# A Fourier filter feeding a soft mixture of experts: loads, stage-1 units and read-backs of the first batches placed by slot, TensorE's order written out

## The chip, the cores and the metric

The kernel runs on one core of one Trainium2 chip. The metric is the device time of one execution in microseconds (us). TensorE is called PE, VectorE DVE, ScalarE ACT, GpSimd POOL; SP is the engine that issues nearly all DMAs.

## The reference

`x` is 8 x 2496 x 256, the filter has 1249 x 256 complex values, and the experts are 8 with 4 slots each and 1024 hidden units. All is float32.

```python
X = np.fft.rfft(x, axis=1)
y = np.fft.irfft(X * (filt_r + 1j * filt_i), n=2496, axis=1)      # each batch, each of 256 columns
t = y.reshape(8 * 2496, 256)
logits = t @ phi                                                   # 19968 x 32
d = softmax of logits over the tokens;  slot_input = d.T @ t       # 32 x 256
slot_out[e] = relu(slot_input[e] @ w1[e]) @ w2[e]
c = softmax of logits over the 32 slots
out = c @ slot_out                                                 # 19968 x 256
```

## The kernel before

A length of 2496 is 39 x 64, and the transform is done in two stages. **Stage 1** works in units of two column blocks of 117 rows: 11 units for each of 8 batches (`split_x` and `s1_unit`). For batch 0 a unit is one float32 matmul of 512 columns (two passes on PE). For the others `split_x` has ACT round x to a reduced float32 (`xh`, L291) and POOL subtract the rest (`xl`, L292), and the unit is three matmuls of the reduced type (L308). The result is copied out of PSUM (`at`, L310 or L312) and written to DRAM (`a_dram`).

**Stage 2** reads `a_dram` back in another layout (`load_ash`, tile `ash`, five buffers) and works in slots: 10 for each batch, 80 in all. Slot n is one `x_unit`: eight PE instructions (L338), two multiplies by the filter on DVE (L352, L353), and an add and a subtract on DVE and POOL (L355, L356). Two slots later `t_unit` transposes the result (L364, copied by ACT at L366) and, every second time, forms logits (L375). Once a group of batches is through, a `chain` takes its logits through an inverse transform and the token softmax and sums `slot_input`; its steps are interleaved with the slots that follow. Batches 0 and 1 are the first group, so that no chain begins before slot 21. After slot 79 come the expert weights' loads, the experts and the combination, whose stores end the kernel.

x comes in chunks of four blocks (two units, 512 KB; six chunks a batch, the last with one unit), in three buffers `xt`; batch 0's x lies in a tile of its own. The filter tables `ff_t` come in ten loads of 256 KB; `sign_tables` multiplies the second half of each by a sign on DVE (L612), with signs made by 20 instructions on PE (`make_signs`, L604).

What sets the order: the program is written slot by slot, and a planner then orders each engine's instructions by a simulated timeline, as far as dependences let it. Where `behind` is called the order is that of the text: for every DMA on SP up to slot 24 (`issue`, `PIN`), and on PE for batch 0's units, the sign matmuls and the matmuls that only keep PE running (`keep_warm`: `WM` at the start, `WK` behind batch 0). ACT, DVE and POOL are ordered by the planner throughout.

The stage-1 units from unit 4 of batch 1 on (`EARLY = 4`; units 0 to 3 go before slot 0) are spread evenly: `slot_of` puts 73 units over 65 slots. `split_next(n + 1)` splits the units of the next slot, and after every second unit `next_x()` issues the next chunk. A batch's read-backs start two slots after its last stage-1 unit at the earliest.

Of the kernel before, what the change touches and what calls it, by code (L numbers as in the profile page):

```python
# [17 lines left out]
BATCH, SEQ, DIM = 8, 2496, 256  # L18
N1, N2 = 39, 64
NT = 20  # L20
NI = 22
NH = 11
# [16 lines left out]
P = 128  # L39
# [6 lines left out]
XB = 3  # L46
AB = 5
EARLY = 4
SPAN = 65
ASH = 5  # L50
LT = 2
HOPS = 2
RT = 1
PR = 2
FB = 1
WM = 1
WK = 2
PIN = 24
FIRST = (0, 2, 6, 10, 14, 18, 22)
PA = 6  # L60
YB = 34
# [4 lines left out]

def slot_of(b, u):

    k = (b - 1) * NH + u - EARLY
    return k * SPAN // ((BATCH - 1) * NH - EARLY) if k >= 0 else -1  # L70


def freq_of(t, c):
# [133 lines left out]
def fft_soft_moe(ctx, tc, x, ff, phi, w1, w2, cst, w1q, out):  # L207
# [24 lines left out]
    def C(name, lo=0, hi=None):  # L232
        o, rows, cols = OFF[name]
        hi = cols if hi is None else hi
        return cst_t[0:rows, o + lo : o + hi]
# [22 lines left out]
    def behind(kind, ins):  # L258
        if kind in queue:
            info = mybir.DependencyInfo(mybir.DependencyClass.NoSync, mybir.DependencyReason.DATA)  # L260
            tc.add_manual_dep(ins.ins, queue[kind].ins.name, info, reason="order of issue")
        queue[kind] = ins

    def issue(dst, src):
        ins = sp.dma_start(dst, src)
        if pinned[0]:
            behind("sp", ins)

    def keep_warm(n):
        for k in range(n):  # L270
            behind("pe", pe.matmul(pw, warm[:, 0:P], warm, start=True, stop=True))
# [10 lines left out]
    def split_x(b, u):  # L282

        if b < FB:
            xhl[b, u] = x0_t[0:KR, 2 * u : 2 * u + 2, :], None
            return
        c, k = divmod(2 * u, XC)
        xs = xts[b, c][0:KR, k : k + 2, :]
        xh = proda.tile([KR, 2, DIM], F32R, tag="xh", name=f"xh{b}_{u}", bufs=3)
        xl = proda.tile([KR, 2, DIM], F32R, tag="xl", name=f"xl{b}_{u}", bufs=3)  # L290
        act.copy(xh, xs)  # L291
        pool_e.tensor_tensor(out=xl, in0=xs, in1=xh.bitcast(F32), op=ALU.subtract)  # L292
        xhl[b, u] = xh, xl
# [3 lines left out]
    def s1_unit(b, u):  # L297
        if u == 0:
            a_dram[b] = scr.tile([N2, QR, DIM], F32, tag="a_dram", name=f"a_dram{b}")
        xh, xl = xhl.pop((b, u))  # L300
        ps = ps_s1.tile([QP, 2, DIM], F32, tag="s1", name=f"s1_{b}_{u}")
        if xl is None:
            at = ypool.tile([QP, 2, DIM], F32, tag="y", name=f"at{b}_{u}")
            behind("pe", pe.matmul(ps, w1q_t, xh, start=True, stop=True))  # L304
        else:
            at = proda.tile([QP, 2, DIM], F32, tag="at", name=f"at{b}_{u}", bufs=AB)
            for n, (w, xx) in enumerate(((w1h, xh), (w1l, xh), (w1h, xl))):
                pe.matmul(ps, w, xx, start=(n == 0), stop=(n == 2))  # L308
        if b == 0 and u % 2 == 1:
            dve.tensor_copy(at, ps)  # L310
        else:
            act.copy(at, ps)  # L312
        k0 = PK * 2 * u
        if u < NH - 1:
            issue(a_dram[b][k0 : k0 + 2 * PK].rearrange("(i j) q d -> (j q) i d", j=PK), at)
        else:
            issue(a_dram[b][k0 : k0 + PK].rearrange("j q d -> (j q) d"), at[:, 0, :])
            issue(a_dram[b][k0 + PK], at[0:QR, 1, :])
# [12 lines left out]
    def x_unit(b, c):  # L331

        t0 = 2 * c
        ash = ashs.pop((b, c))
        ps = ps_x.tile([P, 4, 2, 64], F32, tag="x", name=f"x_{b}_{c}")
        for k in range(2):
            for dh in range(2):
                pe.matmul(  # L338
                    ps[:, 2 * k + dh].rearrange("q r c -> q (r c)"),
                    ash[:, k, dh * P : (dh + 1) * P],  # L340
                    C("b1" if t0 + k else "b0"),
                    start=True,
                    stop=True,
                )
        frv, fiv = (
            ff_t[:, c, k].rearrange("q (p o c) -> q p o c", o=1, c=64).broadcast_to([P, 4, 2, 64]) for k in range(2)
        )
        t2 = prod.tile([P, 4, 2, 64], F32, tag="t2", name=f"t2_{b}_{c}")
        if c % 2 == 0:
            yts[b, c // 2] = prod.tile([P, 2, 4, 2, 64], F32, tag="yt", name=f"yt_{b}_{c}")  # L350
        yt = yts[b, c // 2][:, c % 2]
        dve.tensor_tensor(out=yt, in0=ps, in1=frv, op=ALU.mult)  # L352
        dve.tensor_tensor(out=t2, in0=ps[:, :, ::-1, :], in1=fiv, op=ALU.mult)  # L353
        add = pool_e if b >= PA else dve
        add.tensor_tensor(out=yt[:, :, 1, :], in0=yt[:, :, 1, :], in1=t2[:, :, 1, :], op=ALU.add)  # L355
        pool_e.tensor_tensor(out=yt[:, :, 0, :], in0=yt[:, :, 0, :], in1=t2[:, :, 0, :], op=ALU.subtract)  # L356

    def t_unit(b, c):

        yt = yts[b, c // 2]  # L360
        pt = ps_t.tile([P, 2, 2, P], F32, tag="t", name=f"t_{b}_{c}")
        for k in range(2):
            for dh in range(2):
                pe.transpose(pt[:, k, dh, :], yt[:, c % 2, 2 * k + dh].rearrange("q r c -> q (r c)"), ident)  # L364
        y = ypool.tile([P, 2, DIM], F32, tag="y", name=f"y_{b}_{c}")
        act.copy(y, pt.rearrange("k p h d -> k p (h d)"))  # L366
        ys[b, c] = y
        if c % 2 == 1:
            i = c // 2
            if i == 0:  # L370
                lts[b] = work.tile([P, 5, P], F32, tag="lt", name=f"lt_{b}", bufs=2)
            pl = ps_t.tile([P, P], F32, tag="t", name=f"l_{b}_{i}")
            for dh in range(2):
                for j in range(4):
                    pe.matmul(  # L375
                        pl[32 * j : 32 * j + 32, :],
                        phi_t[:, dh, :],
                        yt[:, j // 2, 2 * (j % 2) + dh].rearrange("q r c -> q (r c)"),
                        start=(dh == 0),
                        stop=(dh == 1),  # L380
                    )
            act.copy(lts[b][:, i, :], pl)

# [209 lines left out]
    def load_tables(c):  # L593
        issue(ff_t[:, c], ff[:, c])
# [25 lines left out]

    xnext = [(b, c) for b in range(1, BATCH) for c in range(6)]

    def next_x():
        if xnext:
            load_x(*xnext.pop(0))

    def split_next(n):
        for b, u in at_slot.get(n, ()):
            split_x(b, u)
            if u % 2 == 1 or u == NH - 1:  # L630
                next_x()

    x0_t = x0p.tile([P, NI, DIM], F32, name="x0_t")
    for i0, i1 in zip(FIRST, FIRST[1:]):
# [11 lines left out]
    for u in range(NH):  # L646
        if u + 1 < NH:
            split_x(0, u + 1)
        s1_unit(0, u)
        if u in (3, 7):  # L650
            next_x()
        if u == 2:
            tc.keep_in_program_order(act.dma_start(cst_t[:, 0:NEAR], cst[:, 0:NEAR]))
        if u == 4:
            tc.keep_in_program_order(act.dma_start(phi_t, phi.rearrange("(h q) e -> q h e", q=P)))
# [4 lines left out]
    def load_to(n):  # L660
        while loads:
            b, c = loads[0]
            if n < max(b * CPB + c - (3 if b < 2 else ASH), slot_of(b, NH - 1) + 2 if b else -3):
                break
            load_ash(*loads.pop(0))

    keep_warm(WK)
    next_x()
    load_tables(next(tabs_next))
    load_to(-3)  # L670
    load_tables(next(tabs_next))
    make_signs()
    for u in range(EARLY):
        split_x(1, u)
        s1_unit(1, u)
        if u % 2 == 1:
            next_x()
            load_to(-2 + u // 2)
    sign_tables(0)
    split_next(0)  # L680
    late = list(tabs_next)
# [42 lines left out]
    for n in range(NS + LT):  # L724
        if n == PIN:
            pinned[0] = False
        if n < NS:
            if late:
                load_tables(late.pop(0))
            load_to(n)  # L730
            if n == CPB + 4:
                issue(cst_t[:, NEAR:FAR], cst[:, NEAR:FAR])
            if n == NS - 2 * CPB:
                behind("sp", sp.dma_start(cst_t[:, FAR:], cst[:, FAR:]))
            if n + 1 < CPB:
                sign_tables(n + 1)
            split_next(n + 1)
            x_unit(*divmod(n, CPB))
        for b, u in at_slot.get(n, ()):
            s1_unit(b, u)  # L740
        if n == last_s1:
            proda_cm.__exit__(None, None, None)
            late_cm, lp = open_pool("late", WL, "right")
            late_pool.append(lp)
            wl = iter(range(WL))
        if n > last_s1 and next(wl, None) is not None:
            load_ws(late_pool[0], "w", 1)
        if n >= LT:
            b, c = divmod(n - LT, CPB)
            t_unit(b, c)  # L750
            if c == CPB - 1 and b in last:
                active.append((last[b], chain(last[b])))
        hop_slot(n)
# [185 lines left out]
```

## Time and profile before

| | us |
|---|---|
| median of 3 runs | 403.64 (401.32 to 404.34) |
| the profiled execution, its own time | 403.31 |
| its span | 401.5 |
| PE busy | 364.6 (91%) |
| DVE busy | 263.6 (66%) |
| ACT busy | 213.1 (53%) |
| POOL busy | 202.1 (50%) |
| granted clock of PE, mean | 0.95 |
| bytes moved by DMA | 109.09 MB, mean 272 GB/s |

The span runs from the first to the last instruction of the profile. Busy time of PE is partly modelled, since matmuls are pipelined. In the rows of single instructions the columns are start, duration, engine, line, operation, and what it writes and reads; a bracket gives the idle time ahead of it and what ended that. `x8` at a row's end means eight instructions merged. "SPq" is the issue of a DMA, not its transfer. `s` is a stage-1 result in PSUM, `x` a stage-2 one.

### The profile page before, as it was taken

What the parts mean: (1) busy time and instruction counts of PE and PEld (TensorE: products, weight loads), DVE (VectorE), ACT (ScalarE), POOL (GpSimd) and SP (SyncE); (2) the same over time, 40 slices, a digit from 0 to 9 for tenths busy, and PEclk for the clock granted to TensorE, in tenths of its full rate; (3) what the DMA queues carried; (4) which work ended last, traced back from release to release, by engine and by line L of the source; (5) the groups of instructions that cost most, each with busy time, mean ns of one, the idle gap of its engine ahead of it and who ended that gap; (6) DMA issues with size and microseconds to landing.
All of it is one profiled execution on the core that took longest, in us unless ns stands there. A gap on an engine that the chain in (4) does not pass through costs nothing.

```text
span 401.5 us, 11478 instructions
## 1 busy us (share of the span) xinstructions
PE 364.6 (91%) x4569; PEld 282.0 (70%) x4569; DVE 263.6 (66%) x460; ACT 213.1 (53%) x453; POOL 202.1 (50%) x229
## 2 busy tenths in 40 slices
PE   8977989998999999999988999999998999998960
PEld 2445767887878876877877688887675834787850
DVE  1223998778689974967899185899349432586640
ACT  2355656676576946655675734444365521475530
POOL 0266688797668674846875535565170004350000
PEclk9998999999999999999999999999999899998555
DMA  8999999899889866976898773352169999299996
GB/s 282 325 307 369 395 362 353 285 297 348 251 271 304 277 216 207 287 237 178 285 315 243 208 241 101 109 153 73 39 225 365 349 258 299 105 414 416 417 416 282
DMA packets 59691, 109.09 MB, mean 272 GB/s; under 512 B 5538, under 2 KB 34338, under 8 KB 57462
## 3 DMA queue, kind: packets, MB, share of 16 engines
q1 hardware_dynamic: 59092, 108.01, 80.0%
q8 instruction: 36, 0.59, 0.6%
q10 hardware_dynamic: 546, 0.35, 0.3%
q14 instruction: 17, 0.14, 0.1%
HBM read 65.60 MB, written 42.74 MB: 270 GB/s over the span
## 4 chain that ended last, share of the span: by engine, by line
PE 62%; DVE 14%; DMA 9%; POOL 4%; issue 4%; ACT 2%; SPq 1%; DVEq 0%; POOLq 0%; ACTq 0%
PE x L338 15%; PE s L308 9%; PE t L364 7%; PE s L558 5%; DMA out<-ob 4%; PE l L375 4%; PE out L890 3%; DMA xt<-in_x 3%; POOL xl L292 3%; PE s L304 3%; PE dd L527 2%; DVE yt L352 2%; DVE t L353 2%; PE o L857 2%; DVE yt L355 2%
## 5 line engine op out<-in xcount | busy, mean ns | idle before, releaser
L292 POOL TENSOR_TENSOR xl<-xt,xh 117x512 fp32r<-117x512 f32 x77 | 104.7, 1372 | 38.9 <-ACT xh L291 35.7
L338 PE MATMUL x<-cst_t,ash 128*128 128x128 f32 x640 | 89.6, 281 | 2.8 <-issue 2.3
L338 PEld LDWEIGHTS x<-cst_t,ash 128*128 128x128 f32 x640 | 81.0, 192 | 12.5 <-issue 7.2
L356 POOL TENSOR_TENSOR yt<-yt,t 128x256 f32<-128x256 f32 x80 | 66.0, 826 | 44.5 <-DVE t L353 35.0
L352 DVE TENSOR_TENSOR yt<-x,ff_t 128x512 f32<-128x512 f32 x80 | 54.6, 682 | 29.2 <-PE x L338 27.6
L312 ACT COPY at<-s 120x512 f32<-120x512 f32 x83 | 48.6, 587 | 27.2 <-PE s L308 16.1
L366 ACT COPY y<-t 128x512 f32<-128x512 f32 x80 | 46.1, 592 | 29.8 <-PE t L364 28.0
L291 ACT CAST xh<-xt 117x512 fp32r<-117x512 f32 x77 | 46.3, 623 | 25.3 <-PE s L308 11.0
L353 DVE TENSOR_TENSOR t<-x,ff_t 128x512 f32<-128x512 f32 x80 | 54.3, 678 | 0.0
L364 PE MATMUL t<-cst_t,yt 128*128 128x128 f32 x320 | 48.5, 276 | 3.2 <-POOL yt L356 2.6
L355 DVE TENSOR_TENSOR yt<-yt,t 128x256 f32<-128x256 f32 x60 | 46.2, 781 | 0.8
L364 PEld LDWEIGHTS t<-cst_t,yt 128*128 128x128 f32 x320 | 36.8, 141 | 10.6 <-POOL yt L356 5.0
L308 PE MATMUL s<-xh,w1h 117*120 117x512 f32 x77 | 36.1, 469 | 4.7 <-ACT xh L291 2.9
L890 PE MATMUL out<-so,st 32*128 32x256 f32 x468 | 35.3, 354 | 2.8 <-ACT ob L895 1.5
L890 PEld LDWEIGHTS out<-so,st 32*128 32x128 f32 x468 | 31.6, 234 | 6.2 <-ACT ob L895 2.6
L895 DVE COPY ob<-out 128x512 f32<-128x512 f32 (+1 forms) x40 | 25.4, 671 | 11.2 <-PE out L890 7.9
L308 PE MATMUL s<-xl,w1h 117*120 117x512 f32 x77 | 32.1, 422 | 0.6 <-POOL xl L292 0.6
L895 ACT COPY ob<-out 128x512 f32<-128x512 f32 (+1 forms) x40 | 21.7, 584 | 17.7 <-PE out L890 12.1
L308 PE MATMUL s<-xh,w1l 117*120 117x512 f32 x77 | 30.6, 398 | 0.0
L355 POOL TENSOR_TENSOR yt<-yt,t 128x256 f32<-128x256 f32 x20 | 15.6, 779 | 26.9 <-DVE t L353 19.9
L375 PE MATMUL l<-yt,phi_t 128*32 128x128 f32 x640 | 27.0, 279 | 1.0 <-issue 0.9
L796 POOL TENSOR_TENSOR c<-cl,r_all 117x352 f32<-117x352 f32 x8 | 6.2, 796 | 41.5 <-DMA cl<-c_dram 33.0
(107 smaller groups left out, 484.1 us busy)
## 6 DMA issues: line engine op xcount, KB each, us to landing
ash<-a_dram SPq DMA_DIRECT2D x80, 256.0 KB
a_dram<-at SPq DMA_DIRECT2D x80, 240.0 KB
xt<-in_x SPq DMA_DIRECT2D x35, 512.0 KB
out<-ob SPq DMA_DIRECT2D x17, 1024.0 KB
w<-in_w SPq DMA_DIRECT2D x64, 256.0 KB
x_t<-in_x SPq DMA_DIRECT2D x5, 512.0 KB
ff_t<-in_ff SPq DMA_DIRECT2D x10, 256.0 KB
out<-ob SPq DMA_DIRECT2D x5, 512.0 KB
```

The source lines that it names most:

```text
L291: act.copy(xh, xs)
L292: pool_e.tensor_tensor(out=xl, in0=xs, in1=xh.bitcast(F32), op=ALU.subtract)
L308: pe.matmul(ps, w, xx, start=(n == 0), stop=(n == 2))
L312: act.copy(at, ps)
L338: pe.matmul(ps[:, 2 * k + dh].rearrange("q r c -> q (r c)"), ash[:, k, dh * P : (dh + 1) * P], C("b1" if t0 + k else "b0"), start=True, st ...
L352: dve.tensor_tensor(out=yt, in0=ps, in1=frv, op=ALU.mult)
L353: dve.tensor_tensor(out=t2, in0=ps[:, :, ::-1, :], in1=fiv, op=ALU.mult)
L355: add.tensor_tensor(out=yt[:, :, 1, :], in0=yt[:, :, 1, :], in1=t2[:, :, 1, :], op=ALU.add)
L356: pool_e.tensor_tensor(out=yt[:, :, 0, :], in0=yt[:, :, 0, :], in1=t2[:, :, 0, :], op=ALU.subtract)
L364: pe.transpose(pt[:, k, dh, :], yt[:, c % 2, 2 * k + dh].rearrange("q r c -> q (r c)"), ident)
L890: nc.tensor.matmul(prs[k][:, mm, :], sts[n][q, hs, c0 : c0 + P], so[q, ho], start=(i == 0), stop=(i == 2))
L895: copy(ob[:, nm * k : nm * (k + 1), :], prs[k])
```

## The change

It places the early work by slot.

- `slot_of`: batch 1's remaining seven units go one to a slot into slots 0 to 6; batch 2's go into slots 8 (two of them) to 17; a later batch b starts min(b, 5) slots before slot 10(b-1) and takes one unit a slot, two in its last. Before, the units of batch 2 lay in slots 6 to 15.
- `next_x(n)`: a chunk is issued in slot n when its first unit is at most two slots away (batches 1 and 2) or four (later ones), behind that slot's table load and read-backs; before, it followed the split that frees its buffer. In the opening the first chunk of batch 1 is issued after unit 5 of batch 0 instead of unit 3, the second after batch 0's last unit instead of unit 7, the third after two table loads and two read-backs.
- The first two early units are computed around the first table and the first read-back; then come a table, a read-back, the signs, a chunk, the other two early units and the third read-back.
- The four early units use one plain float32 matmul each (two passes), without `split_x`'s cast and subtract, and their copies out alternate between ACT and DVE.
- `line`: the matmuls of stage 1, stage 2, the transposes and the logits stand on PE in the order of the text up to slot 20 (`PEPIN`). The chain's are not in that order.
- Batch 2's read-backs may start one slot after its last unit instead of two.
- One more keep-warm matmul at the start (`WM = 2`), none behind batch 0 (`WK` is gone).

```diff
-SPAN = 65
+AHEAD = 5
-WM = 1
-WK = 2
+WM = 2
 PIN = 24
+PEPIN = 20
...
 def slot_of(b, u):
-    k = (b - 1) * NH + u - EARLY
-    return k * SPAN // ((BATCH - 1) * NH - EARLY) if k >= 0 else -1
+    if b == 1:
+        return max(u - EARLY, -1)
+    if b == 2:
+        return NT // 2 - 2 + max(u - 1, 0)
+    return (b - 1) * (NT // 2) + min(u, NT // 2 - 1) - min(b, AHEAD)
...
+    in_line = [True]
+    def line(ins):
+        if in_line[0]:
+            behind("pe", ins)
...
         xs = xts[b, c][0:KR, k : k + 2, :]
+        if b == 1 and u < EARLY:
+            xhl[b, u] = xs, None
+            return
...
-        if xl is None:
+        if b == 0:
             at = ypool.tile([QP, 2, DIM], F32, tag="y", name=f"at{b}_{u}")
-            behind("pe", pe.matmul(ps, w1q_t, xh, start=True, stop=True))
         else:
             at = proda.tile([QP, 2, DIM], F32, tag="at", name=f"at{b}_{u}", bufs=AB)
+        if xl is None:
+            line(pe.matmul(ps, w1q_t, xh, start=True, stop=True))
+        else:
             for n, (w, xx) in enumerate(((w1h, xh), (w1l, xh), (w1h, xl))):
-                pe.matmul(ps, w, xx, start=(n == 0), stop=(n == 2))
-        if b == 0 and u % 2 == 1:
+                line(pe.matmul(ps, w, xx, start=(n == 0), stop=(n == 2)))
+        if xl is None and u % 2 == 1:
             dve.tensor_copy(at, ps)
...
-    def next_x():
-        if xnext:
+    def next_x(n=None):
+        while xnext:
+            b, c = xnext[0]
+            if n is not None and n < slot_of(b, 2 * c) - (2 if b < 3 else 4):
+                break
             load_x(*xnext.pop(0))
+            if n is None:
+                break
     def split_next(n):
         for b, u in at_slot.get(n, ()):
             split_x(b, u)
-            if u % 2 == 1 or u == NH - 1:
-                next_x()
...
         s1_unit(0, u)
-        if u in (3, 7):
+        if u == 5:
             next_x()
...
-            if n < max(b * CPB + c - (3 if b < 2 else ASH), slot_of(b, NH - 1) + 2 if b else -3):
+            if n < max(b * CPB + c - (3 if b < 2 else ASH), slot_of(b, NH - 1) + (1 if b == 2 else 2) if b else -3):
...
-    keep_warm(WK)
     next_x()
     load_tables(next(tabs_next))
+    for u in range(2):
+        split_x(1, u)
+    s1_unit(1, 0)
     load_to(-3)
+    s1_unit(1, 1)
     load_tables(next(tabs_next))
+    load_to(-2)
     make_signs()
-    for u in range(EARLY):
+    next_x()
+    for u in range(2, EARLY):
         split_x(1, u)
         s1_unit(1, u)
-        if u % 2 == 1:
-            next_x()
-            load_to(-2 + u // 2)
+    load_to(-1)
...
+        if n == PEPIN:
+            in_line[0] = False
         if n < NS:
             if late:
                 load_tables(late.pop(0))
             load_to(n)
+            next_x(n)
```

The matmuls of `x_unit` and `t_unit` are wrapped in `line(...)` in the same way.

More of the change, by code (lines that the diff above doesn't have):

```diff
@@ L337, in x_unit @@
             for dh in range(2):
[L338 to L343, printed above, removed]
+                line(
+                    pe.matmul(
+                        ps[:, 2 * k + dh].rearrange("q r c -> q (r c)"),
+                        ash[:, k, dh * P : (dh + 1) * P],
+                        C("b1" if t0 + k else "b0"),
+                        start=True,
+                        stop=True,
+                    )
                 )
@@ L363, in t_unit @@
             for dh in range(2):
-                pe.transpose(pt[:, k, dh, :], yt[:, c % 2, 2 * k + dh].rearrange("q r c -> q (r c)"), ident)
+                line(pe.transpose(pt[:, k, dh, :], yt[:, c % 2, 2 * k + dh].rearrange("q r c -> q (r c)"), ident))
         y = ypool.tile([P, 2, DIM], F32, tag="y", name=f"y_{b}_{c}")
@@ L374, in t_unit @@
                 for j in range(4):
[L375 to L380, printed above, removed]
+                    line(
+                        pe.matmul(
+                            pl[32 * j : 32 * j + 32, :],
+                            phi_t[:, dh, :],
+                            yt[:, j // 2, 2 * (j % 2) + dh].rearrange("q r c -> q (r c)"),
+                            start=(dh == 0),
+                            stop=(dh == 1),
+                        )
                     )
```

## The prediction, made before the change was run

> **What bounds the kernel now.** I read the page's own lines first, then the table by stretches of time, then the chain that ended last, then the order of single instructions in the opening.
>
> ```profile
> span 401.5 us, 11478 instructions
> PE   8977989998999999999988999999998999998960
> PEclk9998999999999999999999999999999899998555
> DMA  8999999899889866976898773352169999299996
> ```
>
> The reader sees TensorE (PE) at nine tenths or more in nearly every slice, and slices 3 and 4 (20 to 40 us) at seven, one of them with a lowered clock. The profiled execution took 403.31 us by its own time: 401.5 of span and 1.8 around it. The median of the three runs shown is 403.64, so the sum below, made against 403.31, stands 0.3 us under it.
>
> ```profile
> 17.20:28.20 11.00, 8.72 (x47) 6.30 (x46) 0.93 (x2) 7.25 (x14) 6.78 (x6) 1.00 0.94 309
> 28.20:39.20 11.00, 7.47 (x36) 5.28 (x35) 3.96 (x9) 5.42 (x10) 7.36 (x7) 0.84 1.02 354
> 39.20:63.80 24.60, 22.52 (x195) 17.90 (x192) 22.87 (x32) 16.12 (x32) 19.66 (x18) 1.00 1.03 379
> 63.80:90.30 26.50, 25.88 (x241) 21.60 (x241) 20.75 (x34) 17.01 (x35) 23.24 (x22) 1.00 0.91 303
> 90.30:290.00 199.70, 192.91 (x2756) 155.94 (x2755) 153.03 (x249) 116.39 (x244) 122.84 (x123) 1.00 0.70 218
> ```
>
> The columns are the length, then PE, weight loads, VectorE (DVE), ScalarE (ACT), GpSimd (POOL), the granted clock, DMA share and GB/s. The cuts are at DVE's first multiply of slots 0, 2, 10 and 20 (a slot is one `x_unit`):
>
> ```profile
> 28.26 0.69 DVE L352 TENSOR_TENSOR yt<-x,ff_t 128x512 f32<-128x512 f32 x1
> 35.05 0.69 DVE L352 TENSOR_TENSOR yt<-x,ff_t 128x512 f32<-128x512 f32 x1 [5.05 <-PE x L338]
> 39.15 0.69 DVE L352 TENSOR_TENSOR yt<-x,ff_t 128x512 f32<-128x512 f32 x1 [1.32 <-PE x L338]
> 63.84 0.68 DVE L352 TENSOR_TENSOR yt<-x,ff_t 128x512 f32<-128x512 f32 x1
> 90.27 0.69 DVE L352 TENSOR_TENSOR yt<-x,ff_t 128x512 f32<-128x512 f32 x1
> ```
>
> So there are three regimes. From 17 to 39 us DMA is full (0.94 and 1.02) and PE works 16.2 of 22 us: slots 0 and 1 take 10.9 us together. Slots 2 to 9 take 24.7 us, 3.09 each, with DVE busy 22.87 of 24.6. From slot 10 on PE is the bound: 25.88 of 26.5 us, and 192.9 of 199.7 after that, with DMA at 0.70. Whatever PE work is ready sooner there comes out sooner, and that stretch runs to the tail, so what the first 64 us give I carry to the end one for one. The ceiling is PE's idle time up to slot 20: 2.3, 3.5, 2.1 and 0.6 us in the four stretches, 8.5 in all, and whatever the lowered clock stretched.
>
> **The opening, where the change acts.**
>
> ```profile
> 15.98 6.03 DMA xt<-in_x
> 25.79 6.30 DMA xt<-in_x
> 15.98 0.91 SPq L265 DMA_DIRECT2D xt<-in_x  x1
> 16.99 3.19 SPq L265 DMA_DIRECT2D a_dram<-at  x4
> 23.97 0.33 SPq L265 DMA_DIRECT2D ash<-a_dram  x1
> 17.21 1.14 ACT L291 CAST xh<-xt 117x512 fp32r<-117x512 f32 x2 [1.35 <-DMA xt<-in_x]
> 18.26 0.58 ACT L312 COPY at<-s 120x512 f32<-120x512 f32 x1
> 27.06 1.16 PE L338 MATMUL x<-cst_t,ash 128*128 128x128 f32 x8
> 32.84 0.49 PE L308 MATMUL s<-xh,w1h 117*120 117x512 f32 x1 [1.54 <-ACT xh L291]
> 33.40 1.62 PE L338 MATMUL x<-cst_t,ash 128*128 128x128 f32 x8
> L292 POOL TENSOR_TENSOR xl<-xt,xh 117x512 fp32r<-117x512 f32 x77 | 104.7, 1372 | 38.9 <-ACT xh L291 35.7
> ```
>
> The first two are pieces of the chain. An x chunk (0.52 MB) is issued at 15.98, in front of the last four writes of batch 0, and the read-back of slot 0 is issued only at 23.97, when those writes have landed. At 25.79 another chunk is issued that lands 6.30 us later. PE waits for its cast (32.84), and slot 1's eight matmuls, which need no x, stand behind that one; they then take 1.62 us, against 1.16 for slot 0's eight at 27.06.
>
> **What the change does there, and the sum.** The second chunk goes behind batch 0's writes. At the 309 GB/s of that stretch 0.52 MB are 1.7 us, so I put the first read-back at 22.3. Casts no longer stand before the copy at 18.26 (1.14 us), because the four early units need none; that lies within the same wait and isn't added. From the issue at 23.97 to DVE's multiply at 28.26 are 4.3 us, so slot 0 starts at 26.6. In the pinned order slot 1 comes after unit (1,4), which needs the third chunk. I place its issue near 24.0, after two read-backs, two tables and two writes. Its landing has bounds from rows: 3.1 us (a read-back of half its size, issued at 23.97, was in use at 27.06) to 6.3. I take 4.0, nearer the short end, since a chunk less is ahead of it. With a cast (0.6, half of the 1.14) and a subtract (1.37) that is 30.0, slot 1 on DVE at 31.4 and slot 2 at 34.2, against 39.15: **-5.0 us**, with bounds -2.7 and -5.9.
>
> ```profile
> 43.83 0.42 DVE L355 TENSOR_TENSOR yt<-yt,t 128x256 f32<-128x256 f32 x1
> 46.35 1.44 DVE L355 TENSOR_TENSOR yt<-yt,t 128x256 f32<-128x256 f32 x1
> 47.72 0.95 DVE L612 TENSOR_TENSOR ff_t<-ff_t,sg 128x256 f32<-128x256 f32 x1
> 44.80 2.71 POOL L292 TENSOR_TENSOR xl<-xt,xh 117x512 fp32r<-117x512 f32 x2
> 47.47 0.92 POOL L356 TENSOR_TENSOR yt<-yt,t 128x256 f32<-128x256 f32 x1
> ```
>
> **Slots 2 to 9.** DVE has the same instructions per slot: two multiplies, an add, a sign table. The add takes 0.42 us alone and 1.44 under a pair of POOL's subtracts; the sign table 0.95 beside POOL's `yt`. That stays, with one subtract per slot at most. Slot 7 has no stage-1 unit now, which takes one 1.37 us subtract away. I take 3.0 us for each of eight slots instead of 3.09: **-0.7 us**. Bounds: 2.6 a slot if no add falls under a subtract (-3.9), and 3.4 if x chunks come late (+2.5).
>
> ```profile
> L308 PE MATMUL s<-xl,w1h 117*120 117x512 f32 x18 | 7.9, 460 | 0.6 <-POOL xl L292 0.6
> L308 PE MATMUL s<-xl,w1h 117*120 117x512 f32 x29 | 12.8, 454 | 0.6 <-POOL xl L292 0.6
> 203.52 1.79 PE x L338 x16
> 205.31 1.40 PE s L308 x6
> 202.64 0.88 PE t L364 x8
> 206.70 0.57 PE l L375 x16
> 110.42 0.86 PE lg L448 x2
> ```
>
> **Slots 10 to 19, and work put off.** The first two rows group the third matmul of a stage-1 unit, up to 62.4 and up to 89.2 us: 18 and 29 units are done before slots 10 and 20. By the new placement it is 14 (4 early, 7 of batch 1, 3 of batch 2) and 25. The other rows, pieces of the chain in the full stretch, give PE's price: 0.89 for a slot's x matmuls, 0.70 for a unit, 0.44 for transposes, 0.29 for logits. With 11 units in ten slots that is 2.39 us a slot; the trace needed 2.64 with 11 units. I take 2.55: **-0.9 us**. Four units put off cost 4 x 0.70 = **+2.8 us** later, where PE is full.
>
> **Edits at nothing.** An early unit in plain float32 costs PE two passes, 0.86 by the row of an equally wide float32 matmul, against 0.70: 0.65 us for four, hidden in the wait for the read-back until 25 us; +0.65 if that cover goes. They take four subtracts (5.5 us) off POOL and four casts (2.3) off ACT before slot 0, where both have time.
>
> ```profile
> 1.45 2.08 PE L271 MATMUL warm_up<-warm 128*128 128x512 f32 x2 [1.45 <-DVE first L639]
> 4.01 13.13 PE L304 MATMUL s<-x_t,w1q_t 117*120 117x512 f32 x22 [0.48 <-DMA w1q_t<-in_w1q]
> 16.97 1.88 PE L271 MATMUL warm_up<-warm 128*128 128x512 f32 x4
> ```
>
> One more warm-up matmul at the start (2.08 us) ends at 5.6 instead of 3.5, so batch 0 may start 1.6 us later; its 22 passes at 0.60 apiece are slower at first, and earlier work may bring full speed sooner by as much. I take 0 (-1 to +1.6). The two warm-ups behind batch 0 (1.88 us) leave a time in which PE has nothing else. Batch 2's read-backs may start at slot 18 and are used at slot 20, two slots (5.1 us) for a write and a read; issue to use was 3.1 for one read, so I take 0, up to +1.5. SP's order: an x load now stands behind that slot's table and read-backs, and no longer waits for a buffer that is still being split; only around slot 22 can it (chunk 0 of batch 4, freed in slot 23), with ash loads five slots ahead behind it: 0.
>
> The sum is -5.0 - 0.7 - 0.9 + 2.8 = -3.8, and 403.31 - 3.8 gives **399.5 us**.
>
> **Rivals.**
>
> *DVE set free (396.3).* The 1.44 us add stood under two subtracts back to back. If the new placement runs subtracts singly, under the multiplies that read PSUM, slots 2 to 9 need 2.6 us: 0.4 x 8 = 3.2 less. For it: one unit per slot, and POOL has 20% idle. Against: a chunk brings two units at once, and the planner still orders POOL. The Trainium skill (SBUF — State Buffer, section "SBUF: two separate sides") says that the pair of ports of VectorE and GpSimd is an exclusive lock for a whole instruction, also for a VectorE instruction with two SBUF inputs; the 1.44 and 0.42 us rows agree.
>
> *The clock falls between batches (402.4).* Without the two warm-ups PE idles from 17.2 until the first chunk is there, near 19.7 (it is issued two units later). After the emptier time before 32.84 the clock was lowered and eight matmuls took 1.62 instead of 0.89. If that happens here, two early units (1.7) and the 20 sign matmuls (2.2, at the x matmuls' 0.11 apiece) take twice, 3.9 more, of which a us is hidden: +2.9. Against it: the stretch from 17.2 to 28.2 us kept 1.00 with PE idle for a fifth of it. The Trainium skill (TensorE: Matmul & The Clock Gate, Part 1) puts the idle window at about 3.4 us; by that a gap of 2.5 keeps the clock, one with a chunk a us later does not.
>
> *Late chunks under a fixed order (slower: 408.5).* For batches 1 and 2 a chunk is issued two slots before its unit. If it takes 6.3 us as at 25.79, plus 2.0 for cast and subtract and 0.95 when POOL is taken, PE has it 9.2 us after issue; two slots and one x unit at 3.0 give 6.9. PE then stands 2.3 us per chunk of two units, with every later x matmul behind it. Nine chunks are used in slots 2 to 17, +21 at worst; but landings should shorten once the tables end at slot 7, so I count four: +9, and 399.5 + 9 is 408.5. It decides from landings over 4 us. For it: DMA share 1.03 up to 63.8. Against: four units less by slot 10 relieve DMA.
>
> **How the numbers follow.** The forecast has 0.60 with its own range 396.5 to 402.5, DVE set free 0.15, the fallen clock 0.13, late chunks 0.12. From 395 to 404 lies nearly all of the first three: 0.86 of the chance, so about 8 in 10 with the unknown costs at their ends. One per cent, 4.0 us, is about what a measurement of this kernel can tell from no change. Below 399.6 lie half of the forecast and the first rival (0.45); within 1% the other half and the fallen clock (0.42); slower the last and a little (0.13).
>
> **What would show it.** Right: DVE's first multiply near 26.6, slot 2 near 34, slot 10 near 58, slot 20 near 83, and 90 to 290 shifted whole, PE full. Read-back of slot 0 issued near 22.3. Wrong: PE waiting in slots 1 to 17 for xh or xl with a landing xt behind them; slots at 2.6 us; slow sign matmuls; or PE idle after slot 20 that eats the lead.

## The result: 421.04 us, 4.3% slower, and the profile after

The changed kernel took 421.04 us (418.94 to 421.79) against 403.74 (401.32 to 404.34): a ratio of 1.043, with a 95% interval of 1.038 to 1.049. The forecast was 399.5 with a range of 395 to 404, so it missed on the side of the third rival, late chunks under a fixed order, priced at 408.5 with a chance of 0.12. Some executions fall into a slower state; the ratios and their intervals are worked out from the runs outside it, so a ratio need not be the quotient of the two medians beside it. The profiled execution took 421.26 by its own time, 419.5 of it span. First the page of the changed kernel: span, PE, PE's clock and DMA in 40 slices, and the x chunks' median from issue to landing.

```profile
span 419.5 us, 11438 instructions
PE   8749687889999999998997999999998999999990
PEclk9997998989999999999998999999999999975555
DMA  8997888697987967797696847733339999299997
xt<-in_x SPq DMA_DIRECT2D x35, 512.0 KB, 5.4
```

PE shows sevens, a six and a four in its first nine slices (up to 94 us); before, slices 3 and 4 were the only sevens of the same stretch. Next, stretches of the changed kernel cut at the same slots as before (0, 2, 10, 20, 79); the columns are those of the prediction's table.

```profile
17.20:26.20 9.00, 7.36 (x36) 4.71 (x36) 1.81 (x3) 2.62 (x5) 0.00 (x0) 1.00 1.00 329
26.20:37.90 11.70, 6.80 (x25) 5.55 (x26) 6.25 (x10) 3.45 (x6) 5.72 (x6) 0.71 0.81 275
37.90:64.80 26.90, 21.16 (x187) 16.25 (x186) 19.87 (x32) 13.35 (x27) 17.66 (x16) 1.00 0.87 278
64.80:101.60 36.80, 31.09 (x244) 24.36 (x243) 19.99 (x33) 19.82 (x40) 24.23 (x23) 0.91 0.75 240
101.60:308.60 207.00, 198.43 (x2788) 159.80 (x2788) 155.28 (x251) 118.92 (x250) 124.78 (x126) 0.99 0.70 220
```

Slots 10 to 19 are the fourth row: 36.8 us, where the kernel before had 26.5. PE is idle for 5.7 us of it (0.6 before), and busy 5.2 us longer for nearly as many matmuls (244 against 241): its clock stood at 0.64 from 70.2 to 75.0 us and at 0.62 from 84.0 to 88.5, each time behind stops, and at 0.91 over the row. DVE, busy 20.75 of 26.5 us there before, now works 19.99 of 36.8: no engine is the bound. DVE's first multiply of slots 0, 1, 2, 10, 12, 16 and 20:

```profile
26.21 0.69 DVE L368 TENSOR_TENSOR yt<-x,ff_t 128x512 f32<-128x512 f32 x1 [0.72 <-PE x L353]
34.84 0.69 DVE L368 TENSOR_TENSOR yt<-x,ff_t 128x512 f32<-128x512 f32 x1 [1.08 <-PE x L353]
37.87 0.68 DVE L368 TENSOR_TENSOR yt<-x,ff_t 128x512 f32<-128x512 f32 x1
64.77 0.69 DVE L368 TENSOR_TENSOR yt<-x,ff_t 128x512 f32<-128x512 f32 x1 [1.14 <-PE x L353]
74.16 0.69 DVE L368 TENSOR_TENSOR yt<-x,ff_t 128x512 f32<-128x512 f32 x1 [5.12 <-PE x L353]
87.98 0.69 DVE L368 TENSOR_TENSOR yt<-x,ff_t 128x512 f32<-128x512 f32 x1 [3.76 <-PE x L353]
101.56 0.69 DVE L368 TENSOR_TENSOR yt<-x,ff_t 128x512 f32<-128x512 f32 x1 [1.53 <-PE x L353]
```

The brackets are the theory in short: DVE stands 5.12 us ahead of slot 12 and 3.76 ahead of slot 16, each time for PE's `x`. What `x` stands behind is seen in slot 13's issues on SP, then ACT's cast and PE's unit:

```profile
75.75 0.34 SPq L268 DMA_DIRECT2D a_dram<-at  x1
76.19 0.45 SPq L268 DMA_DIRECT2D ash<-a_dram  x1
76.72 0.38 SPq L268 DMA_DIRECT2D xt<-in_x  x1
81.97 1.14 ACT L303 CAST xh<-xt 117x512 fp32r<-117x512 f32 x2 [3.38 <-DMA xt<-in_x]
82.64 0.49 PE L322 MATMUL s<-xh,w1h 117*120 117x512 f32 x1 [1.16 <-ACT xh L303]
83.99 0.49 PE L322 MATMUL s<-xl,w1h 117*120 117x512 f32 x1 [0.63 <-POOL xl L304]
```

SP writes a unit's result, reads a slot back, and only then issues the chunk, at 76.72. ACT has waited 3.38 us when it lands, PE's first matmul of it runs 5.9 us after the issue, and the third at 83.99; every later `x` stands behind that one. The chain of waits names the same landings:

```profile
23.56 6.70 DMA xt<-in_x
38.05 6.11 DMA xt<-in_x
62.27 5.65 DMA xt<-in_x
76.72 5.16 DMA xt<-in_x
100.22 6.31 DMA xt<-in_x
```

And between 17 and 100 us, from the table of waits of ACT and PE in the changed kernel (total, times, longest):

```profile
ACT xh L303 <- DMA xt<-in_x: 21.0, 9, 5.8
PE s L322 <- ACT xh L303: 11.2, 6, 4.8
PE s L322 <- POOL xl L304: 5.1, 8, 0.9
```

The same in the kernel before:

```profile
ACT xh L291 <- DMA xt<-in_x: 6.5, 5, 1.7
PE s L308 <- ACT xh L291: 2.9, 3, 1.5
```

PE waits 16.3 us for casts and subtracts in the changed kernel, against 2.9 for casts and 0.6 for subtracts in the kernel before. SP itself waits too. These are its waits for ACT's copy of a stage-1 result (`at`, which SP then writes) between 17 and 100 us, first in the changed kernel, then in the kernel before:

```profile
SPq L268 <- ACT at L326: 35.3, 18, 4.8
SPq L265 <- ACT at L312: 4.1, 6, 1.8
```

By SP's order, which is that of the text, lateness can so feed itself: a late chunk makes a late unit, the unit a late write, and the next read-back and the next chunk stand behind that write.

### The profile page after: what moved, and what is told of

Same layout as the page of the kernel before. It is cut to its first block, busy times and chain, and to the rows that moved or that the text cites. A ratio compares the mean times of both kernels' runs of the same rounds, so it can differ in the third digit from the quotient of the medians.

```text
span 419.5 us, 11438 instructions
## 1 busy us (share of the span) xinstructions
PE 375.5 (90%) x4563; PEld 289.3 (69%) x4563; DVE 264.5 (63%) x462; ACT 209.7 (50%) x447; POOL 194.5 (46%) x225
## 4 chain that ended last, share of the span: by engine, by line
PE 67%; DMA 10%; DVE 10%; issue 4%; ACT 3%; POOL 3%; SPq 1%; DVEq 0%; POOLq 0%; ACTq 0%
PE x L353 14%; PE s L322 9%; PE out L917 8%; DMA xt<-in_x 7%; PE t L380 6%; PE s L576 4%; PE l L392 4%; PE v L439 3%; PE s L319 3%; POOL xl L304 2%; DVE d L502 2%; PE lg L466 2%; PE dd L545 2%; PE h L867 2%; PE u L520 1%
## 5 line engine op out<-in xcount | busy, mean ns | idle before, releaser
L304 POOL TENSOR_TENSOR xl<-xt,xh 117x512 fp32r<-117x512 f32 x73 | 96.9, 1336 | 33.0 <-ACT xh L303 28.2
L353 PE MATMUL x<-cst_t,ash 128*128 128x128 f32 x640 | 94.1, 289 | 2.1 <-issue 1.3
L353 PEld LDWEIGHTS x<-cst_t,ash 128*128 128x128 f32 x640 | 84.3, 200 | 15.2 <-issue 9.6
L303 ACT CAST xh<-xt 117x512 fp32r<-117x512 f32 x73 | 44.2, 620 | 43.9 <-DMA xt<-in_x 25.0
L326 ACT COPY at<-s 120x512 f32<-120x512 f32 x81 | 47.3, 584 | 35.2 <-PE s L322 18.9
L380 PEld LDWEIGHTS t<-cst_t,yt 128*128 128x128 f32 x320 | 38.1, 141 | 9.5 <-POOL yt L372 2.0
L917 PE MATMUL out<-so,st 32*128 32x256 f32 x468 | 38.2, 404 | 1.0 <-ACT so L895 0.5
L917 PEld LDWEIGHTS out<-so,st 32*128 32x128 f32 x468 | 35.6, 284 | 3.4 <-DVE ob L922 1.2
L322 PE MATMUL s<-xl,w1h 117*120 117x512 f32 x73 | 30.9, 424 | 5.2 <-POOL xl L304 5.1
L322 PE MATMUL s<-xh,w1l 117*120 117x512 f32 x73 | 29.5, 404 | 0.0
```

Source lines behind the costliest of these rows:

```text
L322: line(pe.matmul(ps, w, xx, start=(n == 0), stop=(n == 2)))
L353: pe.matmul(ps[:, 2 * k + dh].rearrange("q r c -> q (r c)"), ash[:, k, dh * P : (dh + 1) * P], C("b1" if t0 + k else "b0"), start=True, st ...
L380: line(pe.transpose(pt[:, k, dh, :], yt[:, c % 2, 2 * k + dh].rearrange("q r c -> q (r c)"), ident))
L917: nc.tensor.matmul(prs[k][:, mm, :], sts[n][q, hs, c0 : c0 + P], so[q, ho], start=(i == 0), stop=(i == 2))
```

## The experiments

Three theories were open: **L**, chunks issued too late; **P**, PE's fixed order itself; **D**, units put off to where PE is full. Medians of the kernel before were 403.2 to 404.2 on these chips; each ratio is against it.

**Issue the chunks earlier.**

```diff
-  if n is not None and n < slot_of(b, 2 * c) - (2 if b < 3 else 4):
+  if n is not None and n < slot_of(b, 2 * c) - 4:    # e1: four slots for all
+  ... - (3 if b < 3 else 4):                         # e11: three for batches 1 and 2
```

> The changed kernel with one number altered: chunks of batches 1 and 2 are issued four slots before their first unit instead of two. Theory L (late chunks: a chunk takes about 6 us from issue to landing, two slots ahead are too short, and everything behind its unit in PE's fixed order waits): most of the 17 us comes back, 400 to 408 us. Rival P (the fixed order of PE itself costs, whenever chunks come): 417 or more. Rival D (batch 2's units are put off too far, the work is missing later): 417 or more.

> The changed kernel with chunks of batches 1 and 2 three slots ahead instead of two. L: between the 421 of two slots and the 408.3 of four; a slot is 2.5 to 3 us, and chunks landed 2 to 5.8 us after ACT was free for them, so most of it: 409 to 414. If the loss were a matter of the order of issues on SP and not of the time ahead: still 418 or more.

Four slots ahead: 408.31 us, 1.011 (1.004 to 1.018), just above the 400 to 408 expected. Three: 411.38, 1.017 (1.011 to 1.023). Two, the change: 421.04. Most of the loss goes with two more slots of lead, and all else of the change stayed. Slots 10 to 19, from DVE's first multiply of slot 10 to that of slot 20, took 36.8, 30.9 and 27.7 us with two, three and four slots of lead.

**Undo the fixed order; do it alone.** `PEPIN = 0` in the change, and `line` with `PEPIN = 20` in the kernel before.

> The changed kernel with PE's order fixed only up to slot 0 instead of slot 20; chunks as late as in the change. L: the planner can put other work ahead of a late unit, but ACT, POOL and SP still stand behind the chunk, so part of the loss stays: 408 to 416. P: about 403, the whole loss is gone. D: 417 or more.

> The kernel before with one part of the change: stage-1, stage-2, transpose and logit matmuls in the order of the text up to slot 20; chunks and units as before. L: 401 to 406, since the chunks come as early as before. P: 414 or more. D: 402 to 405.

Without the fixed order the change took 414.49, 1.027 (1.020 to 1.034); the order alone 401.67, 0.996 (0.992 to 1.000). So P alone costs nothing. With late chunks the order adds some 6.5 us, and without it most of the loss stays. These 6.5 us do not lie in slots 10 to 19, which take 38.1 us without the order: e2 is 5.6 us ahead of the change at slot 2, 2.2 at slot 20 and 7.7 at slot 79. So it does not take a unit that holds up the `x` matmuls behind it on PE to make those ten slots long. SP's order, which e2 keeps, is the likelier link: SP waits 31.2 us for `at` there, and 33.6 in e3, the next run, against 4.1 in the kernel before. No run freed SP's order with late chunks, so this is not shown.

**Late chunks alone, and the change without them.** e3 gives the kernel before `next_x(n)` by slot; e8 gives the change the old placement back:

```diff
-  while xnext: ... n < slot_of(b, 2 * c) - (2 if b < 3 else 4) ...
+  if xnext: load_x(*xnext.pop(0))       # after each second split, as before
...
-        if u == 5:
+        if u in (3, 7):
```

> The kernel before with one part of the change: chunks from the third on (fourth chunk of batch 1 onward) are issued by slot, two slots ahead of the unit for batches 1 and 2 and four for later ones, instead of behind the split that frees a buffer; units, PE's order and the opening stay as before. L: slower, 407 to 416. P and D: as before, 402 to 405.

> The changed kernel without its x placement: chunks follow the splits that free their buffers, and the opening's chunks stand where they stood before. Units' slots, PE's order, early units and warm-ups as in the change. L: the whole 17 us are gone, 399 to 404. D: 407 or more. If the rest of the change is worth what I predicted for it without the earlier read-back: about 401.

e3 took 415.38, 1.030 (1.022 to 1.037): late chunks alone make the kernel before some 12 us slower. e8 took 408.38, 1.012 (1.005 to 1.019): 12.7 better than the change, with slots 10 to 19 back at 26.9 us, but it missed its 399 to 404. Something else costs about 1%, and D was next.

**The third chunk earlier still; plain float32 alone.** e5 is e1 with a second `next_x()` ahead of the tables; e6 is the kernel before with the four early units in plain float32.

> The run with chunks four slots ahead, and the third chunk of batch 1 issued right behind the second, ahead of the first table and read-back. L (the rest of the loss, 4.5 us, also comes from a late chunk: the third is issued at 23 us, and slots 0 and 1 stand 6.6 us apart): 1.5 to 4 us less than the 408.3 of that run, 404 to 407. D (the rest is stage-1 work put off to slots where PE is full): unchanged, 408 or more, even if slot 1 comes earlier.

> The kernel before with one part of the change: the four early units of batch 1 in plain float32, without cast and subtract. Prediction's step: costs nothing, 403 to 404.5 (PE's 0.65 us lies in the wait for the first read-back). If ACT or POOL held up the opening: 401 to 403.

e5 took 407.96, 1.010 (1.005 to 1.014): slot 1 began at 31.92 us instead of e1's 33.64, and the end did not move. e6 took 403.99, 1.003 (0.999 to 1.008): float32 in the wait for the read-back costs nothing that these runs can tell from no change.

**The new slots alone, and by halves.** e7 is the kernel before with the new `slot_of`; e9 has it for batches 1 and 2 alone, e10 for batch 3 and on; e14 is e8 with batch 2 two slots earlier.

```diff
     if b == 2:
-        return NT // 2 - 2 + max(u - 1, 0)
+        return NT // 2 - 4 + max(u - 1, 0)     # e14
```

> The kernel before with one part of the change: the units' slots, and batch 2's read-backs allowed one slot after its last unit. Chunks follow the splits as before. L: 402 to 406, the placement of units does no harm while chunks come early; the prediction's own term puts +2.8 us on four units put off, against 0.7 to 1.6 saved. D: 408 to 412, the rest of the loss that chunks four slots ahead left.

> The kernel before with the new slots for the units of batches 1 and 2 alone (and batch 2's read-backs one slot after its last unit); later batches keep the old spread. All new slots together cost 5 us. If the cost is the work put off in the first 20 slots (four units, 2.8 us, and the time that PE then lacks it): 406 to 409. If it is the later batches' placement: 402 to 405.

> The kernel before with the new slots for batches 3 to 7 alone, batches 1 and 2 as before. If the cost of the new slots is work put off in the first 20 slots: 402 to 405. If it is the later batches' placement, with two or three units in one slot at a batch's end: 406 to 409.

> The change with chunks as before, and batch 2's units two slots earlier than in the change (slots 6 to 15 instead of 8 to 17; its read-backs two slots after the last unit, as before). Batch 1's and the later batches' units stay as in the change. With batch 2's units late this was 408.4. If the cost of the new slots is batch 2 alone: 400 to 404. If it is batch 1's one unit a slot or the later batches: 406 or more.

e7: 408.82, 1.012 (1.006 to 1.018), so D is real and not bound to the chunks. e9: 407.04, 1.011 (1.005 to 1.017). e10: 405.9, 1.002 (0.998 to 1.006), no difference that can be told. On the kernel before, the loss goes with batches 1 and 2, where batch 2's read-backs now come just ahead of slot 20. From e9's chain, the read-backs of slot 19 and of slot 20, then DVE's multiplies of these slots:

```profile
78.93 5.86 DMA ash<-a_dram
90.44 2.67 DMA ash<-a_dram
```

```profile
86.03 0.69 DVE L356 TENSOR_TENSOR yt<-x,ff_t 128x512 f32<-128x512 f32 x1 [3.70 <-PE x L342]
94.35 0.69 DVE L356 TENSOR_TENSOR yt<-x,ff_t 128x512 f32<-128x512 f32 x1 [4.92 <-PE x L342]
```

Slot 19, 2.6 us in the kernel before, takes 8.3 here. In e7, with all the new slots, it takes 6.2, yet e7 reaches slot 20 3.4 us ahead of the kernel before and falls behind only after it, 3.3 us at slot 79; so e9 does not show where e7 loses. And e14, with those units two slots earlier, still took 407.27, 1.007 (1.002 to 1.012), so batch 2's delay isn't the whole of it.

**Keep what is good.** e12 is e8 with the old `slot_of` (and batch 2's read-backs two slots after its last unit): the old slots and chunks, with the new opening, the float32 units and PE's fixed order to slot 20. e13 adds the late chunks to it, e15 sets `SPAN = 60`.

> The kernel before with the parts of the change that did no harm so far: the opening's order of units, tables and read-backs, plain float32 for the early units, PE's order fixed up to slot 20, warm-ups as in the change; units' slots and chunks as before. Theory (late chunks and units put off are the whole loss): 398 to 403, not slower than before. If the opening's order or the early units cost something that the others hid: 404 or more.

> The mix (opening, early units in float32, PE's order fixed to slot 20; units' slots as before) with chunks from the fourth of batch 1 on issued by slot, two slots ahead. The 17 us of the change fell from 421 to 408.4 when only the chunks were put back. If late chunks cost the same without the put-off units: 400.6 + 12.6, 411 to 416. If a late chunk hurts only where units are put off as well: 403 to 408.

> The mix with all stage-1 units spread over 60 slots instead of 65, so each comes earlier (the last in slot 59), which also opens the weight buffers five slots earlier. If put-off units cost because PE lacks work later, units brought forward may give a little: 397 to 400. If the spread is already early enough, or DMA, full up to 64 us, can't bring chunks sooner: 400 to 404.

e12 took **400.58 us, 0.993 (0.990 to 0.996): it beats both kernels,** the kernel before by 0.7%. Its slots 2 and 20, and the stretch of slots 10 to 19:

```profile
36.39 0.68 DVE L365 TENSOR_TENSOR yt<-x,ff_t 128x512 f32<-128x512 f32 x1
85.67 0.69 DVE L365 TENSOR_TENSOR yt<-x,ff_t 128x512 f32<-128x512 f32 x1 [0.68 <-PE x L350]
```

```profile
60.00:85.70 25.70, 25.41 (x239) 21.25 (x238) 22.25 (x34) 17.80 (x38) 23.40 (x22) 1.00 0.96 322
```

It reaches slot 20 4.6 us ahead of the kernel before, PE busy 25.41 of 25.7 us, and of that lead some 3 us are left at the end. e13 took 416.42, 1.027 (1.021 to 1.033): late chunks cost 14 to 16 us on this kernel too. e15 took 402.24, 0.994 (0.990 to 0.998), no further gain.

**Where do the new slots lose after slot 20?** PE stands there at times for what the profile calls issue, with nothing released. These rows of e8 carry the longest one, and the clock behind it:

```profile
98.38 0.37 PE L392 MATMUL l<-yt,phi_t 128*32 128x128 f32 x1 [3.29 <-issue]
```

```profile
94.00:98.00 4.00, 1.09 (x61) 0.96 1.05 387
98.00:102.00 4.00, 3.62 (x58) 0.50 0.66 260
```

(The second table is of PE alone: length, busy, clock, DMA share, GB/s.) Three runs put 64 or 96 very small matmuls behind batch 0's units, into e8 (e16, e17) and into e12 (e18):

```diff
     next_x()
+    for k in range(32):                      # e17: 48; a float32 matmul counts twice
+        behind("pe", pe.matmul(pw[0:32, 0:32], warm[:, 0:32], warm[:, 0:32], start=True, stop=True))
```

> The change with its old chunk placement (408.4 us) and 64 more very small PE matmuls (32 by 32) behind batch 0, where PE stands 2.2 us. In the profiles the long standstills of PE after slot 20 that nothing releases come behind the same number of matmuls in every kernel: 710 to 716, 1717 to 1724, 2121 to 2130. Theory (PE's instructions come in blocks over the full DMA queues, some 128 matmuls with their weight loads to a block): the 64 count too, so the standstills come at the same totals, 64 matmuls earlier in the work, or half a block later (838, 1847, 2250 in all); the time moves by several us, 403 to 412. Rival (they belong to the work that is done there): they stay at the same places of the work, at totals of 774, 1783, 2187, and the time stays 408 to 409.

> As the kernel with 64, but 96 matmuls more. Theory: standstills at totals of 710, 1719, 2123 or one block of 128 later, so another place of the work again, 403 to 412. Rival: same places of the work, totals of 806, 1815, 2219, 408 to 409.

> The mix of old slots and old chunks with the new opening (400.6 us) and the same 64 small matmuls. Theory: its short standstills (0.6 at 710, 2.1 at 2123) move too, and with them what follows: 399 to 406. Rival: 400.6 to 401, standstills at 774 and 2187.

Each side was half right. The standstill of some 2.4 us that follows 128 small `u` matmuls stayed with them: at totals of 2121 matmuls in e8, 2185 with 64 more, 2217 with 96. Two others kept to a count. e8's of 3.29 us at 710 came at 839 in e16 and, with 32 matmuls more, again at 839 in e17, at another place of the work; e8's of 0.44 at 2596 came at 2725 in both. One went: e8's of 2.17 us at 1717 has no counterpart of 0.4 us or more in either. First e16, then e17:

```profile
101.29 0.82 PE L353 MATMUL x<-cst_t,ash 128*128 128x128 f32 x5 [0.60 <-issue]
248.21 0.31 PE L439 MATMUL v<-cst_t,lsb 128*32 128x66 f32 x5 [2.56 <-issue]
```

```profile
103.99 0.45 PE L439 MATMUL v<-cst_t,lsb 128*32 128x66 f32 x17 [2.90 <-issue]
253.70 0.77 PE L439 MATMUL v<-cst_t,lsb 128*32 128x66 f32 x37 [2.73 <-issue]
```

By the times, the standstills are not the whole of the new slots' price: e16 406.53, 1.011 (1.003 to 1.019), and e17 410.38, 1.020 (1.013 to 1.027), stay above the kernel before with their standstills elsewhere. The 3.85 us between the two are not clear of their intervals, so what a standstill costs in the end is not shown. e18 took 400.83, 0.993 (0.989 to 0.996), as e12. Part of the price is seen in slots 25 to 34, which begin at 102.15 us in e12 and in e16. The stretch, the third matmul of a unit, and a wait of PE; e12:

```profile
102.15:135.00 32.85, 32.67 (x433) 26.19 (x432) 31.89 (x52) 24.18 (x52) 22.17 (x21) 1.00 0.81 252
L319 PE MATMUL s<-xl,w1h 117*120 117x512 f32 x11 | 4.4, 401 | 0.0
```

and e16:

```profile
102.15:138.55 36.40, 34.35 (x442) 27.74 (x441) 34.78 (x51) 26.28 (x58) 24.27 (x22) 1.00 0.83 264
L322 PE MATMUL s<-xl,w1h 117*120 117x512 f32 x14 | 5.6, 401 | 0.0
PE l L392 <- ACT y L382: 1.9, 1, 1.9
```

The stretch is 3.55 us longer in e16. PE is busy 1.7 us longer, with two to three units more (14 of the third matmul against 11, 13 against 11 of the first two), and the rest is one wait of 1.9 us for ACT. The kernel before has 13 units there and takes 33.8, so the units are only a part of it. At slot 79 e16 is 6.0 us behind e12. What makes that wait was not tried, and so the rest of the new slots' price stays open.

## Why the prediction was wrong, point by point

**The opening** (-5.0, bounds -2.7 to -5.9) gave -1.3 at slot 2. Its first half held: the read-back of slot 0 went out at 21.46 (22.3 predicted) and slot 0 began at 26.21 (26.6). The third chunk was issued at 23.56 (24.0 predicted), but the landing that I took as 4.0 us took 6.70, past the 6.3 of the row that I had shown and not chosen. PE then stood 4.78 us, and slot 1's eight matmuls took 1.91 us at a lowered clock (0.50 from 30.9 to 37.0 us). From the unit's third matmul, at 32.31, to slot 1's multiply it took 2.5 us where I had 1.4. My sum had no term for the clock, and that is why the gain fell short of the bound of -2.7 too:

```profile
21.46 0.33 SPq L268 DMA_DIRECT2D ash<-a_dram  x1
30.95 0.78 PE L322 MATMUL s<-xh,w1h 117*120 117x512 f32 x1 [4.78 <-ACT xh L303]
32.89 1.91 PE L353 MATMUL x<-cst_t,ash 128*128 128x128 f32 x8
```

**Slots 2 to 9** (-0.7, up to +2.5) took 26.9 us against 24.7: +2.2, inside the bound for late chunks.

**Slots 10 to 19** is the step that failed: -0.9 predicted, 36.8 us against 26.4 measured, +10.4. I made that term from PE's work alone and gave it no bound for late chunks, though the same two slots of lead hold there. In the rival I had the mechanism, but cut nine chunks to four because "landings should shorten once the tables end at slot 7". They did not: 5.65, 5.16 and 6.31 us at 62, 77 and 100, with the DMA share down to 0.75. I had also left out PE's lowered clock behind such stops (PE was busy 5.2 us longer there) and the writes of late units that stand ahead of the next chunk on SP. PE's fixed order, which the rival named, is not needed for the loss: e3 has none. All nine at 2.3 us was the "+21 at worst"; the pairs of runs measured 12.7 (the change against e8), 15.8 (e13 against e12; 13.8 by their ratios) and some 12 (e3). "It decides from landings over 4 us" was right, and every chunk's landing that I had a row for was over 4: a chance of 0.12 was far too small.

**Work put off** (+2.8) was too small: slots 20 to 79 took 207.0 us against 200.2, +6.8. Four more units are done there, as predicted (51 of the first matmul against 47), but PE was busy 5.0 us longer instead of 2.8, and idle 1.8 us longer. The granted clock of 0.99 against 1.00 can make some 2 us of the busy time, by my estimate from the length of the stretch; the idle time is waits and standstills. The claim that a lead is carried to the end one for one fails with the new slots: e8 reached slot 20 5.3 us ahead of the kernel before and slot 79 7.5 behind. With the old ones it nearly holds: e12 was 4.6 us ahead at slot 20 and 3.8 at slot 79. The four parts, -1.3 + 2.2 + 10.4 + 6.8 = 18.1, meet the difference of the spans, 18.0.

**Read-backs of batch 2** (0, up to +1.5) were too cheap: slot 19 took 8.3 us in e9, though 3.6 in the changed kernel itself, against 2.6 before.

**Edits at nothing** held: float32 early units (e6), and the second warm-up, with batch 0's units through at 16.04 instead of 17.14. **The fallen clock between batches** did not come: PE stood 2.21 us there, and the 20 sign matmuls took 2.44.

```profile
18.24 1.95 PE L319 MATMUL s<-xt,w1q_t 117*120 117x512 f32 x4 [2.21 <-DMA xt<-in_x]
20.03 2.44 PE L622 MATMUL sgn<-cst_t 128*128 128x128 f32 x20
```

The clock fell at the later, longer stop of 4.78 us. The Trainium skill (TensorE: Matmul & The Clock Gate, Part 1) puts the idle window at about 3.4 us; 2.21 and 4.78 lie on its two sides, and so far the trace agrees. It does not for single stops further on: the clock of 0.64 from 70.2 us came behind stops of 1.78 and 0.83 us with two matmuls between, that of 0.62 from 84.0 behind 1.16 and 0.63.

**DVE set free** found no ground: in the changed kernel DVE was busy 19.87 of 26.9 us in slots 2 to 9 and was not the bound. In e12 slots 2 to 9 took 23.6 us, 2.95 each, near the 3.0 of the forecast.

## What to carry to other kernels

Count the lead of a load in microseconds from its place in the issuing queue to the engine that needs it (here some 5 to 7 for the landing, 2 for cast and subtract), and divide by the shortest slot; a lead counted in slots shrinks as the slots get faster. Look, too, at what stands ahead of the load in that queue: if it is a write that waits for the load before, one late load delays the next. An order written out for PE alone was worth little here (0.4%, not clear of nothing) and cost some 6.5 us together with late loads, so set it only with loads that are early enough. When a rival's mechanism decides from a threshold that every row at hand already passes, it is the forecast and not a rival.

## What was not expected of the hardware

The five landings of 512 KB chunks in the changed kernel's chain took 5.2 to 6.7 us from issue, whether the DMA share was 1.0 or 0.75. They are those that something waited for; over the kernel the profile gives 4.2 to 6.3 us with a median of 5.4. None came down to the 4.0 that I had hoped for.

PE stands 0.4 to 3.3 us at certain counts of matmuls (710, 839, 1086, 1214, 1719, 2596 and 2725 in the stretches from the start to each standstill, over several kernels: about 1, 2, 1, 4, 7 and 1 times 128 apart). Not every standstill keeps to them: e1 has one of 1.95 us and e5 one of 1.28 at 767, and e6 one of 0.67 at 1127. The page of e8 shows a queue that fits:

```profile
q8 instruction: 36, 0.59, 0.6%
```

36 packets of 16 KB for 4563 matmuls and as many weight loads are 127 of each to a packet; e16 to e18, with 64 and 96 matmuls more, have 37 packets. The Trainium skill (Runtime: NRT & Kernel Launch, section "Instruction fetch mechanics") says that an engine's instructions come in blocks of 16 KiB, 256 instructions, over a DMA queue, and that this is mostly hidden. The packets and most of the counts agree with the blocks, but the 3.29 us in e8, if they are such a block, were not hidden. That a block is late because the other queues are full (DMA share 1.05 ahead of the 3.29 us) is a guess from these rows that no run tried.
